# First q, k, v gradient tiles of a dense stage fetched while attention ends, weights partly issued by GpSimd, and copies of the last forward pair on ScalarE

## The chip, the cores and the metric

The kernel runs on one core of a Trainium2 chip. The metric is the device time of one execution in microseconds (us). The kernel before was run four times: 2415.22, 2419.77, 2419.97 and 2423.10 us, with a median of 2419.87.

## What is computed

The reference runs four residual layers forward over a sequence of 2048 rows with width 640, and then the gradients of all inputs for a given output gradient. Layers 0 and 2 are linear attention (A), layers 1 and 3 are sliding-window softmax attention with a window of 256 (B). The two A layers share weights, as do the two B layers. There are 32 heads of 20 columns.

```python
def _A_ref(x, wqkv, wo):
    ...
    pq, pk = phi(q), phi(k)
    kv = jnp.einsum("bhsd,bhse->bhde", pk, v)
    ...
    o = num / den
    return (lambda x, *d: x.transpose(*d))(o, 0, 2, 1, 3).reshape(B, S, D) @ wo

def _B_ref(x, wqkv, wo):
    ...
    mask = (idx[:, None] - idx[None, :] >= 0) & (idx[:, None] - idx[None, :] < W)
    scores = jnp.where(mask[None, None], scores, -1e9)
    p = _softmax(scores, axis=-1)
    o = jnp.einsum("bhqk,bhkd->bhqd", p, v)
    return (lambda x, *d: x.transpose(*d))(o, 0, 2, 1, 3).reshape(B, S, D) @ wo
...
x = x + _A_ref(_layernorm(x, axis=-1), A_wqkv, A_wo)
x = x + _B_ref(_layernorm(x, axis=-1), B_wqkv, B_wo)
x = x + _A_ref(_layernorm(x, axis=-1), A_wqkv, A_wo)
x = x + _B_ref(_layernorm(x, axis=-1), B_wqkv, B_wo)
```

The outputs are the last x and the gradients of the input, of the two qkv weights and of the two output weights.

## The kernel before

The sequence is cut into 16 tiles of 128 rows. Everything is unrolled in Python. Most instructions on an engine may be put in an order that the compiler's scheduler chooses, but a transfer that is "pinned" stays behind what was written before it for the same engine.

**Stages, in order of time.** The q, k, v products of layer 0 come first. Then come two forward pairs (`seg_pair`, layers 0 and 1, then 2 and 3). A pair runs the attention scores of layer B as the backbone: 16 row tiles with 8 groups of 4 heads each. For every unit, TensorE makes the scores (L412), ScalarE the exponentials (L418), GpSimd masks the edges (L421, L424), and TensorE multiplies by v (L440). Between them a plan feeds pieces of the row-wise work: `mix`, `proj1`, `qkv`, `proj2`. In the last pair two more are in the plan: `fetch_g` transposes a tile of the output gradient on TensorE and copies it from PSUM into `gT`; `do` multiplies it by the transposed weight (L811). In the middle of each row tile `flip_some` also transposes 128 columns of a weight on TensorE, copies them from PSUM into `flip_t` (L201) and stores them to HBM as `WT_d`, for the backward stages. `steady[0]` is true from the first unit of the row loop up to the last, and false before and after. The PSUM banks of all this row-wise work come from one pool of four (`d` in the profile), so a transpose on TensorE waits until an earlier bank has been copied out.

Then comes the backward pass: attention of layer 3 (about 832 to 1211 us), the dense stage of layers 3 and 2 (1211 to 1500), attention of layer 1 (1500 to 1971), the dense stage of layers 1 and 0 (1971 to 2224), and the rest of the weight gradients (to the end).

**Attention backward** (`seg_attention_bwd`) runs 8 groups of 4 heads by 16 row tiles, 128 units, and five steps more to empty its pipeline. In step s, TensorE makes the scores of unit s (L903), ScalarE its exponentials (L917), GpSimd masks them (L921, L925), and VectorE makes ds of the unit before (L937). Half of ds is transposed by a DMA from SP into `dsT`, the other half on TensorE (L947) and copied out (L950). In step s the products of unit s - 5 (L963) read dsT and give the q, k, v gradients `dqkv_o`, which are evacuated (L996) and stored to `dqkv` in HBM, four row tiles in one transfer from GpSimd's queue. A filler puts weight-gradient products of other layers (L1039) into the same PSUM bank; when its last one has been handed out it calls `late` (layer 3) or `done` (layer 1). These give the filler's SBUF pools back and queue the 26 weight tiles of the next dense stage: 15 of `WT`, 5 of `WoT`, 6 of `mbdT`, each 160 KB.

**Queues.** SP issues the loads and all DMA transposes (L152) in the order written. `drip(n)` takes n waiting loads off a list and pins them on SP at the start of a step: 3 in the first 16 steps, then 2, then 4 from step 112 on. `flush` issues waiting stores from GpSimd's queue (both show as L125).

**The dense stage** (`seg_dense_bwd`) starts when attention has ended. What is left in the list is issued, then per row tile `fetch` loads five tiles two steps ahead, the first of them a DMA transpose of `dqkv` into `dqkvT`; `dh0` and `dh1` multiply it by `WT` in 30 matmuls (L771); ScalarE and VectorE make the layer-norm gradient `car` (L779 to L788); TensorE transposes it; `dO` follows. The pool of `dqkvT` lies in memory that attention used, so the first transpose also waits for attention's last evacuation.

Of the kernel before, what the change touches and what calls it, by code (L numbers as in the profile page):

```python
# [14 lines left out]
BF = mybir.dt.bfloat16  # L15
F32 = mybir.dt.float32
P = 128
# [6 lines left out]
class Kern:  # L24
# [111 lines left out]
        while self.stores:  # L136
            self.dma(*self.stores.pop(0), self.nc.gpsimd)

    def drip(self, n, pin=True, queue=None):
        queue = self.queue if queue is None else queue  # L140
        while queue and (n > 0 or callable(queue[0])):
            x = queue.pop(0)
            if callable(x):
                x()
                continue
            x = self.dma(*x, self.nc.sync)
            if pin:
                self.tc.keep_in_program_order(x)
            n -= 1
# [339 lines left out]
    def seg_pair(self, l, acc, on_tail=None):  # L489

        nc, TT, H, G = self.nc, self.TT, self.H, self.G
        with ExitStack() as st:
# [7 lines left out]
            last = l + 2 > 3  # L500
# [8 lines left out]
            for i in range(2):  # L509
                s = pW.tile([P, 2 * H * HP], BF, name=f"qk_slab{i}")  # L510
# [3 lines left out]
            for i in range(5):  # L514
                s = pW.tile([P, H * HP], BF, name=f"v_slab{i}")
# [6 lines left out]
            steady = [False]  # L522
# [10 lines left out]
            bank = Bank()  # L533
# [39 lines left out]
            if last:  # L573
                WoT = pW.tile([P, self.DT, self.D], BF, name="WoT1")
                gr, gT, o3 = {}, {}, {}

            def fetch_g(t):
                if t == 0:
                    self.tr(WoT, self.Wo[1])
                if t == 0:  # L580
                    gr[0] = self.rows_in(pw.tile([P, self.D], BF, name="g_ld"), self.grad_out[0:P, :])
                if t + 1 < TT:
                    gr[t + 1] = self.rows_in(pw.tile([P, self.D], BF, name="g_ld"),
                                            self.grad_out[(t + 1) * P:(t + 2) * P, :])
                gT[t] = pw.tile([P, self.DT, P], BF, name="gT", bufs=1)
                self.flip(gr.pop(t), self.DT, gT[t], bank, [nc.vector.tensor_copy])
                yield 640

            def do(t):
# [23 lines left out]

            def nc_eng():
                turn[0] += 1
                return nc.vector.tensor_copy if steady[0] or turn[0] % 2 else nc.scalar.copy

            def pieces():
# [35 lines left out]
            n = len(units)  # L654
            AHEAD, LAG = 1, 2
            evs, it, done = {}, None, 0
            for u in range(-AHEAD, n + LAG):
# [9 lines left out]
                if 0 <= u < n:  # L667
# [3 lines left out]
                    for i, f in enumerate((1 / 3, 2 / 3, 1)):  # L671
                        self.flush()
                        while done < work * (g + f) / G:
                            w = next(it, None)
# [27 lines left out]
            if last:  # L702
                drain(fetch_g(TT - 1))
# [148 lines left out]
        self.tc.add_manual_dep(x.ins, y.ins.name, mybir.DependencyInfo(  # L852
            mybir.DependencyClass.NoSync, mybir.DependencyReason.DATA), reason="order")

    def seg_attention_bwd(self, l, fill):


        nc, T, TT, D, G = self.nc, self.T, self.TT, self.D, self.G
# [6 lines left out]
        with ExitStack() as st:  # L865
# [141 lines left out]
            n = len(units)  # L1007
            for s in range(n + JL):
                self.att_step = s
                self.flush()  # L1010
                self.drip(3 if s < TT else 2 if s < n - TT else 4)
                self.drip(2 if s < TT else 3, True, self.queue2)
                if s < n and units[s][1] == 3 and units[s][0] + 1 < G:
                    load(units[s][0] + 1)
                a, b2, c = s, s - PL - 1, s - PL
                bank = ahead() if 0 <= s - JL < n else None
                sa = scores(a, 0, "QT", "KT") if a < n else None
                pb = scores(b2, 1, "dOT", "VT") if 0 <= b2 < n else None
                if a < n:
                    expo(a, 0, sa)  # L1020
                if 0 <= b2 < n:
                    dscore(b2, 1, pb)
                if bank:
                    job(s - JL, *bank)
                sb = scores(a, 1, "QT", "KT") if a < n else None
                pa = scores(c, 0, "dOT", "VT") if 0 <= c < n else None
                if a < n:
                    expo(a, 1, sb)
                if 0 <= c < n:
                    dscore(c, 0, pa)  # L1030
                if 0 <= b2 < n:
                    flip(b2)
# [125 lines left out]
        return dmbd, dmbdT  # L1158

    def dense_weights(self, l, pool):  # L1160
        w = [self.load_w(pool, 1, "WT"), self.load_w(pool, 0, "WoT"), pool.tile([P, 6, self.D], BF, name="mbdT")]
        self.later([(w[2][:, k, :], self.sv[l - 1]["mbdT"][:, k, :]) for k in range(6)])
        return w

    def seg_dense_bwd(self, l, w, mid):

        nc, TT, D, DT, H, HD = self.nc, self.TT, self.D, self.DT, self.H, self.HD
# [3 lines left out]
        with ExitStack() as st:  # L1171
# [7 lines left out]
            with ExitStack() as s2:  # L1179
                p1 = self.pool(s2, "b1")  # L1180
                p1w = self.pool(s2, "b1w", 2)
                pl = self.pool(s2, "b1l", 3)
                WTB, WoTA, mbdT = w
                WTA = WoTB = None
                pps = self.pool(s2, "ps", 2, PSUM)
                pbd = self.pool(s2, "psb", 1, PSUM)
# [5 lines left out]
                dT, hn, g, o, pq, ps, gT, dN, dNT, dq = ({} for _ in range(10))  # L1192

                def fetch(t):
                    dT[t] = pl.tile([P, self.QTT, P], BF, name="dqkvT")
                    self.tr(dT[t], self.dqkv_d[l][:, t, :])
                    hn[t] = self.rows_in(pl.tile([P, D], BF, name="hn_ld"), self.hn_d[l][:, t, :])
                    g[t] = self.rows_in(pl.tile([P, D], BF, name="g_ld"), self.g_d[l][:, t, :])
                    o[t] = self.rows_in(pl.tile([P, D], BF, name="o_ld", bufs=4), self.o_d[a][:, t, :])
                    pq[t] = self.rows_in(pl.tile([P, D], BF, name="pq_ld", bufs=5), self.tm(sv["pq"])[:, t, :])  # L1200
# [65 lines left out]
            with ExitStack() as s2:  # L1266
                p2 = self.pool(s2, "b2")
                p2w = self.pool(s2, "b2w", 2)
                pl = self.pool(s2, "b2l", 3)
                pps = self.pool(s2, "ps", 3, PSUM)  # L1270
                hn, o, pk, pkT, vT, ps, gT, dkv, dkvT = ({} for _ in range(9))
# [123 lines left out]
    def run(self):  # L1395
        s_att = self.ctx.enter_context(ExitStack())
        with ExitStack() as st:
# [18 lines left out]
            for l in (0, 2):  # L1416
                self.seg_pair(l, acc, None if l == 0 else tail)
                self.drip(len(self.queue))
                if l == 0:
                    sA.close()  # L1420
        own = 6
        s_wg, last = ExitStack(), []
        with ExitStack() as s2:
            w = []

            def late():
                s_own.close()
                w.extend(self.dense_weights(3, self.pool(s2, "pre", side="right")))

            def mid():  # L1430
                s2.close()
                self.load_A(1)
                c0 = own * 12 * DH
                jobs = [(self.hn_d[3], self.dqkv_d[3], (c0, self.QT), self.part[1][0]),
                        (self.o_d[3], self.g_d[3], (0, self.D), self.part[1][1]),
                        (self.hn_d[2], self.dqkv_d[2], (0, self.QT), self.part[0][0]),
                        (self.o_d[2], self.g_d[2], (0, self.D), self.part[0][1])]
                last.append(self.fill_dram(s_wg, jobs, done))

            s_own = ExitStack()  # L1440
            self.seg_attention_bwd(3, self.fill_own(3, s_own, own, late))
            s_end, s3 = self.ctx.enter_context(ExitStack()), ExitStack()
            w1 = []

            def done():
                s_wg.close()
                w1.extend(self.dense_weights(1, self.pool(s3, "pre", side="right")))
            self.seg_dense_bwd(3, w, mid)
        fill = last[0]
        self.seg_attention_bwd(1, fill)  # L1450
        if fill.left:
            with ExitStack() as s2:
                ps = self.pool(s2, "wgp", 2, PSUM)
# [9 lines left out]
        last = []  # L1463
# [69 lines left out]
```

## Time and profile before

| | |
|---|---|
| median of 4 runs | 2419.87 us |
| profiled execution | 2414.3 us, span 2412.6 us |
| mean granted TensorE clock | 0.931 |
| TensorE (PE) busy | 2145.1 us, 89% |
| VectorE (DVE) busy | 1552.8 us, 64% |
| ScalarE (ACT) busy | 1242.6 us, 52% |
| GpSimd (POOL) busy | 1147.6 us, 48% |
| moved by DMA | 472.07 MB, 196 GB/s |

Stage by stage (window sums of the same execution):

| window, us | stage | PE busy | DVE | ACT | POOL | DMA share |
|---|---|---|---|---|---|---|
| 600 to 660 | last forward pair | 54.4 | 50.6 | 43.7 | 49.3 | 0.95 |
| 1160 to 1206 | attention of layer 3 ends | 40.1 | 32.1 | 29.1 | 19.8 | 0.81 |
| 1206 to 1216 | seam to dense | 4.1 | 2.8 | 1.5 | 1.9 | 0.56 |
| 1940 to 1976 | attention of layer 1 ends, seam | 21.6 | 17.9 | 13.5 | 10.6 | 0.92 |
| 1976 to 2115 | dense, first half | 126.7 | 89.5 | 48.1 | 50.4 | 0.73 |

A line of the profile names the engine, the line of the kernel (L771 is line 771), the operation and its tiles as out<-in. Busy time is not a limit in itself: an engine at 80% with a queue in fixed order can be late for the others, and one at 50% on which everything waits can set the time. The slices of the page are a fortieth of the span, 60.3 us each. SPq and POOLq are the queues in which SP and GpSimd issue transfers; the time shown for such an instruction is that of issuing it.

### The profile page before, as it was taken

What the parts mean: (1) busy time and instruction counts of PE and PEld (TensorE: products, weight loads), DVE (VectorE), ACT (ScalarE), POOL (GpSimd) and SP (SyncE); (2) the same over time, 40 slices, a digit from 0 to 9 for tenths busy, and PEclk for the clock granted to TensorE, in tenths of its full rate; (3) what the DMA queues carried; (4) which work ended last, traced back from release to release, by engine and by line L of the source; (5) the groups of instructions that cost most, each with busy time, mean ns of one, the idle gap of its engine ahead of it and who ended that gap; (6) DMA issues with size and microseconds to landing.
All of it is one profiled execution on the core that took longest, in us unless ns stands there. A gap on an engine that the chain in (4) does not pass through costs nothing. (4 is left out here: it accounts for less than half of the span.)

```text
span 2412.6 us, 68804 instructions
## 1 busy us (share of the span) xinstructions
PE 2145.1 (89%) x27568; PEld 1494.4 (62%) x27672; DVE 1552.8 (64%) x3022; ACT 1242.6 (52%) x1971; POOL 1147.6 (48%) x1779
## 2 busy tenths in 40 slices
PE   7879999879988699999889798889999979889989
PEld 4645565545555357777667575567777757667445
DVE  6657777567888568778756586556666656646112
ACT  4447777637767557777623353545666633333000
POOL 4447676557877536666433243445555533311000
PEclk9989999989999759999799998789999989989999
DMA  8599898488989798889798695999989999497797
GB/s 254 149 186 216 185 196 189 128 181 203 215 190 199 196 242 164 143 146 167 160 220 219 143 251 167 250 213 188 186 182 201 177 206 232 124 269 203 198 279 210
DMA packets 814817, 472.07 MB, mean 196 GB/s; under 512 B 609664, under 2 KB 781872, under 8 KB 814496
## 3 DMA queue, kind: packets, MB, share of 16 engines
q1 hardware_dynamic: 772880, 336.42, 67.8%
q0 software_dynamic: 41616, 131.25, 17.0%
q8 instruction: 216, 3.54, 0.6%
q14 instruction: 105, 0.86, 0.1%
HBM read 187.07 MB, written 161.19 MB: 144 GB/s over the span
## 5 line engine op out<-in xcount | busy, mean ns | idle before, releaser
L937 DVE SCALAR_TENSOR_TENSOR ds<-sp,e 128x768 bf16<-128x768 f32 (+2 forms) x512 | 463.0, 906 | 244.6 <-PE sp L903 151.3
L917 ACT ACTIVATE e<-sp 128x768 bf16<-128x768 f32 (+2 forms) x512 | 395.1, 776 | 257.7 <-PE sp L903 182.8
L418 ACT ACTIVATE e<-s 128x1024 bf16<-128x1024 f32 x360 | 364.8, 1024 | 115.6 <-PE s L412 69.7
L412 PE MATMUL s<-qbd,ring 128*128 128x512 bf16 x616 | 211.6, 387 | 6.6 <-ACT e L418 2.3
L921 POOL TENSOR_SCALAR_AFFINE_SELECT e<-e 128x512 bf16<-128x512 bf16 x256 | 164.6, 643 | 110.4 <-ACT e L917 101.2
L1039 PEld LDWEIGHTS <-wg_l 128*128 128x128 bf16 x2800 | 187.5, 99 | 42.9 <-DVE wg_o L1045 12.8
L903 PE MATMUL sp<-KT,QT 32*128 32x384 bf16 (+2 forms) x1024 | 186.0, 348 | 17.9 <-ACT e L917 10.9
L421 POOL TENSOR_SCALAR_AFFINE_SELECT e<-e 128x512 bf16<-128x512 bf16 x256 | 170.3, 667 | 47.9 <-ACT e L418 46.3
L903 PE MATMUL sp<-VT,dOT 32*128 32x384 bf16 (+2 forms) x1024 | 182.3, 344 | 9.5 <-ACT e L917 6.2
L1378 PE MATMUL wg<-wg_r,wg_l 128*128 128x480 bf16 (+1 forms) x960 | 177.4, 347 | 7.0 <-DMA wg_r<-dqkv 5.3
L1039 PE MATMUL acc<-wg_r,wg_l 128*128 128x160 bf16 x1840 | 157.3, 239 | 22.1 <-DMA wg_l<-o 6.1
L267 PE MATMUL d<-W,ln_hnT 128*128 128x320 bf16 x960 | 151.9, 307 | 25.5 <-ACT ln_hnT L730 8.7
L368 PE MATMUL d<-W,ln_hnT 128*128 128x480 bf16 x640 | 156.9, 377 | 4.8 <-DMA ln_hnT<-ln_hn 1.9
L771 PE MATMUL d<-WT,dqkvT 128*128 128x320 bf16 x960 | 144.7, 305 | 9.6 <-DMA dqkvT<-dqkv 5.0
L424 POOL TENSOR_SCALAR_AFFINE_SELECT e<-e 128x512 bf16<-128x512 bf16 x224 | 149.0, 665 | 8.7 <-ACT e L418 7.8
L1378 PEld LDWEIGHTS <-wg_l 128*128 128x128 bf16 x960 | 94.6, 99 | 89.7 <-issue 12.0
L440 PEld LDWEIGHTS <-e 128*128 128x128 bf16 x2880 | 109.9, 96 | 60.6 <-POOL e L421 22.8
L925 POOL TENSOR_SCALAR_AFFINE_SELECT e<-e 128x512 bf16<-128x512 bf16 x224 | 142.9, 638 | 0.0
L947 PE MATMUL tp<-ident,ds 128*128 128x128 bf16 x1440 | 137.1, 235 | 5.6 <-DVE ds L937 3.5
L267 PEld LDWEIGHTS <-ln_hnT 128*128 128x128 bf16 x960 | 94.3, 100 | 76.2 <-issue 20.6
L963 PEld LDWEIGHTS <-dsT 128*128 128x128 bf16 x2880 | 93.9, 98 | 69.7 <-issue 45.5
L440 PE MATMUL d<-v_slab,e 128*128 128x42 bf16 (+1 forms) x2880 | 116.2, 180 | 22.5 <-POOL e L421 19.2
(200 smaller groups left out, 4528.6 us busy)
## 6 DMA issues: line engine op xcount, KB each, us to landing
qkvT<-ring POOLq DMA_DIRECT2D x32, 512.0 KB, 5.3
dqkv<-dqkv_o POOLq DMA_DIRECT2D x64, 240.0 KB, 4.4
wg_r<-dqkv SPq DMA_DIRECT2D x64, 240.0 KB, 4.5
hn<-ln_hn SPq DMA_DIRECT2D x64, 160.0 KB, 2.9
qk<-qk_flat POOLq DMA_DIRECT2D x64, 160.0 KB, 4.0
qk_r<-qk SPq DMA_DIRECT2D x32, 320.0 KB, 4.2
hn_ld<-hn SPq DMA_DIRECT2D x64, 160.0 KB, 3.7
dqkv<-dkv_t POOLq DMA_DIRECT2D x32, 320.0 KB, 4.2
```

Source lines behind the costliest of these rows:

```text
L267: nc.tensor.matmul(ps, lhsT=hnT[:, k, :], rhs=W[:, k, ci * HD:(ci + 1) * HD], start=(k == 0), stop=(k == self.DT - 1))
L368: nc.tensor.matmul(ps, lhsT=hnT[:, k, :], rhs=W[:, k, ci * 480:(ci + 1) * 480], start=(k == 0), stop=(k == self.DT - 1))
L412: nc.tensor.matmul(ps[:, i, :], lhsT=self.ring_at(ring, 1, kt)[:, g, :], rhs=self.qbd[b % 2][:, g, :, :], start=True, stop=True)
L418: nc.scalar.activation(e[:, 0:i + 1], ps[:, 0:i + 1], ACT.Exp, scale=self.c_att)
L421: nc.gpsimd.affine_select(out=ev, in_=ev, compare_op=ALU.is_ge, fill=0.0, base=0, pattern=[[0, 4], [1, P]], channel_multiplier=-1)
L440: nc.tensor.matmul(ov[:, h % 16:h % 16 + w, :], lhsT=ev[i][:, hh, :], rhs=v[:, h:h + w, 0:DH + 1], start=(i == 0), stop=(i == nkt - 1), sk ...
L903: nc.tensor.matmul(ps[:, j, 0:nkt * P], lhsT=slabs[g][ta][r0:r0 + HP, b * P:(b + 1) * P], rhs=slabs[g][tb][r0:r0 + HP, k0 * P:(k0 + nkt) * P],
L917: nc.scalar.activation(ev[:, 2 * half:2 * half + 2], ps[:, :, 0:nkt * P].rearrange("p h (i k) -> p h i k", k=P), ACT.Exp, scale=c_att)
L921: nc.gpsimd.affine_select(out=ev[:, :, nkt - 1, :], in_=ev[:, :, nkt - 1, :], compare_op=ALU.is_ge, fill=0.0, base=0, pattern=[[0, 4], [-1 ...
L937: nc.vector.scalar_tensor_tensor(out=dv[:, hs], in0=ps[:, :, 0:nkt * P].rearrange("p h (i k) -> p h i k", k=P), scalar=c_att, in1=ev[:, hs ...
L1039: x = self.nc.tensor.matmul(ps[:, 0:w], lhsT=lhs(t), rhs=rhs(t), start=(t == 0), stop=(t == self.TT - 1), skip_group_check=True)
L1378: nc.tensor.matmul(ps, lhsT=lhs[:, tt, rows], rhs=rhs[:, tt, 0:w], start=(tt == 0), stop=(tt == TT - 1))
```

## The change

Three edits:

1. In the last forward pair, `gT` is copied out of PSUM by ScalarE, no longer by VectorE, and so is `flip_t` while `steady[0]` holds. 16 and 15 copies of 128x640 bf16 change their engine.
2. In attention backward, from step 112 on, `drip` issues three loads from SP and then one more from GpSimd's queue, in place of four from SP.
3. The tiles `dqkvT` 0 of layer 3, and 0 and 1 of layer 1, are allocated together with the weights of the dense stage. Their DMA transposes are issued by SP at the start of step 126, two steps before the last unit's scores, ahead of that step's loads. `fetch` then leaves them out for these tiles.

```diff
-    def drip(self, n, pin=True, queue=None):
+    def drip(self, n, pin=True, queue=None, eng=None):
...
-            x = self.dma(*x, self.nc.sync)
+            x = self.dma(*x, eng or self.nc.sync)
...
-                self.flip(gr.pop(t), self.DT, gT[t], bank, [nc.vector.tensor_copy])
+                self.flip(gr.pop(t), self.DT, gT[t], bank, [nc.scalar.copy])
...
             def nc_eng():
                 turn[0] += 1
+                if last and steady[0]:
+                    return nc.scalar.copy
                 return nc.vector.tensor_copy if steady[0] or turn[0] % 2 else nc.scalar.copy
...
-    def seg_attention_bwd(self, l, fill):
+    def seg_attention_bwd(self, l, fill, end):
...
-                self.drip(3 if s < TT else 2 if s < n - TT else 4)
+                if s == n - 2:
+                    end()
+                self.drip(3 if s < TT or s >= n - TT else 2)
+                if s >= n - TT:
+                    self.drip(1, True, None, nc.gpsimd)
...
-        w = [self.load_w(pool, 1, "WT"), self.load_w(pool, 0, "WoT"), pool.tile([P, 6, self.D], BF, name="mbdT")]
+        w = [self.load_w(pool, 1, "WT"), self.load_w(pool, 0, "WoT"), pool.tile([P, 6, self.D], BF, name="mbdT"),
+             [pool.tile([P, self.QTT, P], BF, name=f"dqkvT{i}") for i in range(1 if l == 3 else 2)]]
...
                 def fetch(t):
-                    dT[t] = pl.tile([P, self.QTT, P], BF, name="dqkvT")
-                    self.tr(dT[t], self.dqkv_d[l][:, t, :])
+                    if t < len(ahead):
+                        dT[t] = ahead[t]
+                    else:
+                        dT[t] = pl.tile([P, self.QTT, P], BF, name="dqkvT")
+                        self.tr(dT[t], self.dqkv_d[l][:, t, :])
...
+        def ahead(l, w):
+            for i, x in enumerate(w[3]):
+                self.tr(x, self.dqkv_d[l][:, i, :])
...
-            self.seg_attention_bwd(3, self.fill_own(3, s_own, own, late))
+            self.seg_attention_bwd(3, self.fill_own(3, s_own, own, late), lambda: ahead(3, w))
...
-        self.seg_attention_bwd(1, fill)
+        self.seg_attention_bwd(1, fill, lambda: ahead(1, w1))
```

More of the change, by code (lines that the diff above doesn't have):

```diff
@@ L1182, in seg_dense_bwd @@
                 pl = self.pool(s2, "b1l", 3)
-                WTB, WoTA, mbdT = w
+                WTB, WoTA, mbdT, ahead = w
                 WTA = WoTB = None
```

## The prediction

> **What bounds the kernel now.** I read the page first. Its slices show TensorE busy nearly everywhere and no one engine that is the limit of the whole, so the change has to be judged in the three places that it touches: the last forward pair, and the two seams from attention backward to dense backward (layers 3 and 1).
>
> ```profile
> PE   7879999879988699999889798889999979889989
> DVE  6657777567888568778756586556666656646112
> ACT  4447777637767557777623353545666633333000
> DMA  8599898488989798889798695999989999497797
> ```
>
> The last forward pair lies in slices 9 to 13 (about 545 to 812 us): PE is at 8 to 9 tenths, VectorE at 8, ScalarE at 6 or 7. DMA is at 9 almost everywhere.
>
> The second view is the chain that ended last, around the seam of layer 1.
>
> ```profile
> 1966.35 3.76 DMA dsT<-ds
> ...
> 1970.16 0.82 PE acc L963 x20
> ...
> 1971.10 4.69 DMA dqkvT<-dqkv
> ...
> 1975.93 6.04 PE d L771 x30
> ```
>
> The attention stage ends with the landing of its last dsT transpose (columns: start, length). Then the first tile of the dense stage is asked for, and TensorE stands until it is there. The timeline of PE at the layer-3 seam shows the same hole: the first product of the dense stage is
>
> ```profile
> 1216.11 10.70 PE L771 MATMUL d<-WT,dqkvT 128*128 128x320 bf16 x57 [4.66 <-issue]
> ```
>
> and its transpose was issued at 1211.59. The two holes, 4.66 and 4.96 us, lie on PE, and all that follows hangs on them.
>
> Third, SP's queue in the timeline before the layer-1 seam:
>
> ```profile
> 1945.83 1.76 SPq L125 DMA_DIRECT2D WT<-WT_d  x4
> ...
> 1949.08 2.02 SPq L125 DMA_DIRECT2D WT<-WT_d  x4
> 1951.20 1.78 SPq L152 DMA_TRANSPOSE dsT<-ds  x1
> ```
>
> A step costs SP four weight pieces at about 0.5 us and one transpose at 1.2 to 1.8, in all 3.3 us, while TensorE would step in 2.5 us (L963 at 1942.0, 1944.5, 1947.0, 1949.5). From 1945.8 to the last dsT, issued at 1966.35, SP therefore sets the pace.
>
> Fourth, what PE waits for in the forward window (the waits of PE, 545 to 812):
>
> ```profile
> PE d L728 <- DVE flip_t L201: 7.5, 7, 1.4
> PE d L440 <- POOL e L421: 6.3, 7, 2.0
> PE d L811 <- DVE car L253: 5.2, 5, 1.4
> ```
>
> Columns: total us, times, longest. VectorE being late costs PE more there than anything else.
>
> **What the skill says.** The Trainium skill, "DMA: Bandwidth & Descriptors", section "Issuing engines are not separate DMA queues": all issuing engines feed the same 16 DMA engines, and a second one saves only sequencer time. The trace agrees that the sequencer is worth saving (0.44 to 0.58 us a piece on SP) and warns that little else is: the DMA engines are busy 0.92 of 1940 to 1976. The same page, section "SWDGE vs HWDGE vs iDMA": a plain DMA transpose can't be issued from GpSimd; so only weights can leave SP. "VectorE: DVE Perf Modes", section "Specifications", has ScalarE closer to PSUM; here the copy of 128x640 bf16 out of PSUM takes 476 ns on VectorE (gT) and 692 ns on ScalarE (ln_hnT), so ScalarE is not the faster one, only the freer one.
>
> **The change, part by part.**
>
> *1. Copies to ScalarE.* 16 gT copies and 15 flip_t copies in the steady part go over. VectorE loses 31 x about 0.46 = 14 us, ScalarE gains 31 x 0.692 = 21 us. Over the 267 us that makes VectorE 0.81 to 0.75 and ScalarE 0.71 to 0.79 (window sums). What counts is PE's wait. Around a typical row (flip_t at 576.06) PE had finished its transposes about 2 us earlier, VectorE got to the copy only behind slow qbd copies, bn_stats and ln_mv, and PE then stood 1.19 us because the next flip needs that PSUM bank. ScalarE was idle for 2.35 us just then. So most of the 7.5 us should go, and the freed VectorE brings the car and o_b additions forward by up to 0.9 us a row, perhaps half of their 5.2 + 2.8 us: 11 us of relief. Against it stand the exponentials behind a copy, 0.69 us late each, some of which will reach PE through the GpSimd masks (the 6.3 us row grows). I take 5 us for that: **-6 us**. From both sides: -12 (all waits on VectorE go) to +10 (each copy delays PE by a third of a us).
>
> *2. Weights from GpSimd, layer 3.* 26 weight pieces come 3 + 1 per step from SP and GpSimd, so SP issues some 20. A dsT goes out 0.5 us earlier in a step, and up to 3.5 us over seven if nothing else holds it. PE waits for dsT there at 1173.20 (1.99 us), 1184.87 (2.37) and 1188.18 (0.16): 4.5 us are to be had. But SP also waits 6.1 us for VectorE's ds in 1160 to 1190, and the 4.06 us that four WoT pieces took at 1177.09 looks like a full queue rather than issue cost. **-2 us** (0 to -4.5). GpSimd pays 0.55 us a piece (its own 160 KB stores, g<-car, take 0.55 to 0.60) and has gaps of about 1 us a step: nothing, while those gaps last.
>
> *3. First tile ahead, layer 3.* One transpose (SP 1.3 to 2.9 us) two steps before the end. SP waits for ds between its last nine transposes (20.9 us for 9, against 1.2 of issue), so it fits in; it lands long before 1211. The hole of 4.66 goes. Next in line is the second tile, still fetched after the stage begins: four row loads (2.0 us), then the transpose (4.3 to 5.4 to landing) makes about 7 us, against 6.1 us of PE on the first tile. 0.9 us stays: **-3.8 us**.
>
> *4. The same at layer 1, two tiles.* The hole of 4.96 goes; the third tile has 12 us of PE ahead of it: **-4.9 us**. But here SP is full. Moving six pieces before the last dsT saves 6 x 0.5 = 3.0 us; the two transposes, put ahead of three dsT, cost 2.6 (unblocked) to 5.6 us, and their 2 x 480 KB compete with weights at about 200 GB/s, up to 5 us more for a dsT behind them. I take **+1.5 us** for the end of attention (-1 to +5).
>
> *5. The new wait.* SP's first weight waits for the last gradient store to land,
>
> ```profile
> SPq L125 <- DMA po0w<-wg_o: 2.2, 1, 2.2
> ```
>
> and 0.9 us at layer 3. GpSimd's first piece must wait for the same memory; behind it stand the two affine_selects of that step, and VectorE's ds waits for them: about 2 us late at layer 1. The cover is SP, which from there on is later than that anyway. If SP were quicker than I think, this wait would be what is late next.
>
> The sum is -6 - 2 - 3.8 - 4.9 + 1.5 = **-15.2 us**. The profiled execution took 2414.3 us (span 2412.6); it would become 2399.1. It lies 5.6 us under the median of 2419.87, so on the scale of the median I say **2405**.
>
> **Rivals.** *(a) The copies bring nothing*: PE's waits change their name from VectorE to ScalarE. For it: ScalarE runs exponentials of 1024 ns back to back in many rows. Against it: in the rows at 576, 634, 653, 673 and 736 us it was idle for 0.5 to 2.35 us just before ln_lv. The rest gives -9.2: 2411. *(b) The seams give back what they save*: with DMA at 0.92, prefetched tiles and weights delay the dsT that end the stage (+5 at layer 1, 0 at layer 3). With the copies and the holes -9.7: 2410; without the copies too, 2416. *(c) Slower: ScalarE becomes what PE waits for.* A flip_t copy queues behind ln_lv, which waits for VectorE's ln_mv, and an exponential; PE's next flip then waits up to 1.0 + 0.69 us, in 13 rows 22 us. Less the 9.2 of the seams that is +13: 2433. It decides from 9.2 us, or 0.3 us for each of the 31 copies. The idle ScalarE at those moments speaks against it. *(d) The change doesn't take effect*: the early transposes queue behind something on SP and land no earlier, and the waits pass from one engine to another: 2420, as now.
>
> **Numbers.** Main case 0.60 (its own range 2397 to 2412), (a) 0.17, (b) 0.10, (c) 0.09, (d) 0.04. The range that leaves out 2 in 10 is 2395 to 2418. A change under 0.2%, 4.8 us, can't be told from none here. Faster by more than that: the main case nearly whole (0.58), most of (a) (0.13), half of (b) (0.05), together 0.76. Slower: (c) and a little of (d), 0.11. Within: 0.13.
>
> **What would show it.** Right: no DMA wait ahead of the first L771 product at either seam; WT pieces in POOL's queue at about 0.55 us; flip_t and gT as ScalarE copies of 0.69 us, the PE wait on flip_t much under 7.5 us and the exponentials' wait on PE not much grown; dsT at the end of layer 1 issued within 2 us of before. Wrong: a PE wait of several us on dsT at the end of attention, POOL's affine_selects late with VectorE waiting, or the forward window longer than before with PE waiting for ScalarE.

## The result, and the profile after

| | runs | median, us |
|---|---|---|
| before, same chip | 56 | 2419.65 |
| after | 37 | 2416.35 |

The ratio is 0.9984, with a 95% interval of 0.9973 to 0.9994. Of 2419.65 us that is 3.9 us less (1.5 to 6.5), where 15 were forecast. The profiled execution of after took 2417.2 us (span 2415.4, mean granted TensorE clock 0.933), which is 2.9 us *longer* than that of before. A single profile scatters by several us, so stretches are compared here, not spans, and each stretch over more than one kernel.

The slices of the page are nearly those of before:

```profile
PE   6879999879898689999989797879999979889999
DVE  6657777567877557778766586556666656656212
ACT  4447777647777557777723343545666533333000
DMA  8599898489997799889998695999889999597797
```

**The last forward pair.** The waits of PE from 545 to 812 us, the longest five (total us, times, longest):

```profile
PE d L251 <- DVE o_t L347: 9.8, 8, 2.4
PE d L730 <- DVE o_b L446: 5.9, 4, 2.3
PE d L440 <- DVE car L253: 3.4, 8, 0.7
PE s L412 <- ACT e L418: 2.1, 3, 1.8
PE d L440 <- POOL e L421: 2.0, 4, 0.9
```

The wait on flip_t, 7.5 us before, is gone. So is most of the one on GpSimd. But PE's waits on VectorE add up to 21.3 us, against 18.7 before: other tiles of VectorE's are now what PE stands for, above all o_t, the output of layer A's attention. The timeline of after shows how, in the same place that the prediction had taken as typical (start, length, in brackets the idle time before and what ended it):

```profile
573.78 2.63 DVE L399 COPY qbd<-ring 32x1024 bf16<-32x1024 bf16 x2
...
574.79 0.69 ACT L201 COPY flip_t<-d 128x640 bf16<-128x640 bf16 x1
...
576.45 0.49 DVE L217 BATCH_NORM_STATS2 ln_st<-car 128x6 f32<-128x320 bf16 x1
...
577.46 0.89 DVE L347 TENSOR_TENSOR o_t<-d,rinv 128x320 bf16<-128x320 f32 x2
...
578.00 0.84 PE L251 MATMUL d<-Wo,oT 128*128 128x320 bf16 x5 [1.54 <-DVE o_t L347]
```

The copy is made on ScalarE at 574.79, and nobody waits for it. VectorE still spends 2.63 us in two copies of q into the operand `qbd` of the scores (one takes 0.40 us at its shortest), then does the layer-norm statistics, and only then o_t. PE stands 1.54 us for o_t, where it had stood 1.19 us for flip_t.

**The seam of layer 3.** PE's timeline, first products of the dense stage:

```profile
1211.33 0.70 PE L773 MATMUL d<-WT,dqkvT 128*128 128x320 bf16 x4
1212.68 0.70 PE L773 MATMUL d<-WT,dqkvT 128*128 128x320 bf16 x4
1213.77 3.15 PE L773 MATMUL d<-WT,dqkvT 128*128 128x320 bf16 x22
1221.34 4.76 PE L773 MATMUL d<-WT,dqkvT 128*128 128x320 bf16 x24 [4.42 <-DMA dqkvT<-dqkv]
```

The hole before the first product has gone: the products even start between the last ones of attention. A hole of nearly the same length, 4.42 us, stands ahead of the second tile, which landed 7.3 us after attention's end.

**The seam of layer 1.** SP's queue:

```profile
1947.70 1.21 SPq L152 DMA_TRANSPOSE dsT<-ds  x1
1948.95 1.56 SPq L125 DMA_DIRECT2D WT<-WT_d  x3
1950.61 5.72 SPq L152 DMA_TRANSPOSE dqkvT<-dqkv  x1
1956.43 2.21 SPq L152 DMA_TRANSPOSE dsT<-ds  x1
1958.69 1.52 SPq L125 DMA_DIRECT2D WT<-WT_d  x3
1960.31 2.23 SPq L152 DMA_TRANSPOSE dsT<-ds  x1
1962.58 3.12 SPq L152 DMA_TRANSPOSE dqkvT<-dqkv  x1
```

The three weights of a step now cost about 1.5 us, as meant. But the early transposes hold SP for 5.72 and 3.12 us, and the compiler's scheduler (the planner, from here on), free to move them since they are not pinned, put one of them ahead of five dsT and the other ahead of three (the last three dsT are issued behind the lines shown). On PE two of the groups of products that need a dsT are late:

```profile
1963.62 0.55 PE L965 MATMUL acc<-qk_r,dsT 128*128 128x40 bf16 x12 [6.56 <-DMA dsT<-ds]
...
1971.74 0.56 PE L965 MATMUL acc<-qk_r,dsT 128*128 128x40 bf16 x12 [3.95 <-DMA dsT<-ds]
```

And the chain that ended last goes on, behind the end of attention (start, length, what):

```profile
1973.82 3.26 DMA dsT<-ds
...
1977.79 6.67 PE d L773 x49
1984.45 4.78 issue
1989.24 0.69 PE t L730 x5
```

No transfer stands before the first product any more, but PE waits 4.78 us before the first transpose of `car`. What it waits for is in the timeline of the other engines:

```profile
1980.95 0.79 ACT L781 ACTIVATE dh_s<-d,rs 128x640 f32<-128x640 f32 x1 [5.02 <-PE d L773]
...
1982.77 3.30 POOL L1151 MEMSET dmbd<- 128x3840 bf16 x1 [3.21 <-issue]
1983.01 3.24 DVE L1254 TENSOR_SCALAR dphi<-pq_ld 128x640 bf16<-128x640 bf16 x1 [4.78 <-DMA g_ld<-g]
1986.17 0.81 DVE L784 CUSTOM_DVE_ANT_0 dh_junk<-dh_s,hn_ld 128x640 bf16<-128x640 f32 x1
...
1988.02 0.32 DVE L1254 TENSOR_SCALAR dphi<-pq_ld 128x640 bf16<-128x640 bf16 x1
```

ScalarE's dh_s is ready at 1981.8. The next step for `car` is dh_junk on VectorE, but the planner put dphi ahead of it: an operation for a later piece of the tile, which waits for the row load pq_ld (landed at 1982.88; the mark in the line names a load that had landed earlier) and then takes 3.24 us beside a memset of GpSimd's. The next one of the same shape takes 0.32.

### The profile page after: what moved, and what is told of

Its sections match the earlier page's. It is cut to its first block, busy times and chain, and to the rows that moved or that the text cites. A ratio compares the mean times of both kernels' runs of the same rounds, so it can differ in the third digit from the quotient of the medians.

```text
span 2415.4 us, 68820 instructions
## 1 busy us (share of the span) xinstructions
PE 2145.5 (89%) x27566; PEld 1495.0 (62%) x27672; DVE 1553.0 (64%) x2991; ACT 1261.1 (52%) x2002; POOL 1155.3 (48%) x1791
## 4 chain that ended last, share of the span: by engine, by line
PE 37%; DMA 9%; issue 6%; DVE 4%; POOL 3%; SPq 3%; ACT 2%; DVEq 0%; ACTq 0%; POOLq 0%
PE acc L965 7%; PE acc L1045 7%; PE d L773 6%; PE wg L1388 5%; PE sp L905 5%; PE tp L949 3%; SPq L125 2%; POOL do_o L753 2%; DMA dsT<-ds 2%; PE t L730 2%; ACT e L919 1%; DVE ds L939 1%; DVE car L790 1%; PE d L738 1%; DMA dqkvT<-dqkv 1%
## 5 line engine op out<-in xcount | busy, mean ns | idle before, releaser
L1045 PEld LDWEIGHTS <-wg_l 128*128 128x128 bf16 x2800 | 189.5, 100 | 46.1 <-DVE wg_o L1051 16.1
L905 PE MATMUL sp<-VT,dOT 32*128 32x384 bf16 (+2 forms) x1024 | 181.2, 342 | 10.1 <-ACT e L919 6.4
L440 PEld LDWEIGHTS <-e 128*128 128x128 bf16 x2880 | 110.3, 97 | 59.3 <-POOL e L421 18.0
L965 PE MATMUL acc<-qk_r,dsT 128*128 128x40 bf16 (+1 forms) x2880 | 118.4, 181 | 21.4 <-DMA dsT<-ds 20.8
```

The source lines that it names most:

```text
L905: nc.tensor.matmul(ps[:, j, 0:nkt * P], lhsT=slabs[g][ta][r0:r0 + HP, b * P:(b + 1) * P], rhs=slabs[g][tb][r0:r0 + HP, k0 * P:(k0 + nkt) * P],
L965: x.append(nc.tensor.matmul(acc[:, hh * DH:hh * DH + w], lhsT=lhsT, rhs=rhs(rname, g, t, hh, w), start=(i == 0), stop=(i == len(s) - 1), s ...
L1045: x = self.nc.tensor.matmul(ps[:, 0:w], lhsT=lhs(t), rhs=rhs(t), start=(t == 0), stop=(t == self.TT - 1), skip_group_check=True)
```

## The experiments

The marks used: "end" is the last product of attention backward, counted from the end of the last filler product, which is the last work that the change leaves alone; "car" is the first transpose of `car` on PE, from the end of attention or, as "tail", from that filler product. All are us of one profile. Every kernel was timed against before on the same chip; ratios carry their 95% interval. The kernels e1, e2, e3 and e5 share one chip, e7, e9, e10 and e11 a second, e12, e13 and e14 a third, so a difference between two ratios may cross chips. Three ratios rest on few executions (6 of e7, 9 of e10, 10 of e13), the others on 14 or more.

| kernel | ratio | layer 3: end, car, tail | layer 1: end, car, tail | PE waits for dsT, layer 1 |
|---|---|---|---|---|
| before | 1 | 54.5, 15.8, 70.3 | 31.7, 15.1, 46.8 | 8.8 |
| after | 0.9984 (0.9973 to 0.9994) | 50.5, 12.0, 62.6 | 36.5, 11.5, 47.9 | 12.4 |
| e1_copies | 0.9984 (0.9959 to 1.0009) | 51.7, 15.6, 67.3 | 30.4, 15.1, 45.5 | 7.8 |
| e2_ahead | 0.9996 (0.9983 to 1.0010) | 51.7, 13.6, 65.3 | 34.7, 9.8, 44.5 | 7.0 |
| e3_gpsimd | 0.9982 (0.9969 to 0.9995) | 49.4, 17.0, 66.4 | 28.0, 15.5, 43.6 | 5.2 |
| e5_dphi | 0.9968 (0.9953 to 0.9983) | 49.4, 12.6, 62.0 | 37.0, 7.1, 44.1 | 12.2 |
| e4_pinned | 0.9970 (0.9954 to 0.9986) | 49.4, 12.8, 62.2 | 35.2, 10.1, 45.4 | 11.1 |
| e11_actq | 1.0023 (1.0009 to 1.0037) | 53.3, 12.1, 65.4 | 40.4, 10.3, 50.7 | 2.1 |
| e7_late_dphi | 0.9947 (0.9927 to 0.9967) | 48.2, 11.5, 59.7 | 29.6, 12.8, 42.4 | 6.5 |
| e9_late | 0.9947 (0.9933 to 0.9962) | 47.7, 11.6, 59.3 | 30.8, 13.3, 44.1 | 4.5 |
| e10_second | 0.9954 (0.9933 to 0.9975) | 48.8, 14.1, 62.9 | 27.9, 12.5, 40.3 | 5.8 |
| e12_late_nocopies | 0.9968 (0.9950 to 0.9986) | 50.0, 12.0, 62.0 | 29.3, 13.4, 42.7 | 6.5 |
| e13_bytes | 0.9957 (0.9933 to 0.9980) | 48.7, 12.4, 61.1 | 32.6, 12.9, 45.5 | 9.1 |
| e14_late_gT | 0.9961 (0.9946 to 0.9977) | 48.7, 12.8, 61.5 | 31.6, 13.0, 44.5 | 7.1 |

### One part alone

*e1_copies*: the kernel before with the two edits to the copies, and nothing else of the change.

```diff
-                self.flip(gr.pop(t), self.DT, gT[t], bank, [nc.vector.tensor_copy])
+                self.flip(gr.pop(t), self.DT, gT[t], bank, [nc.scalar.copy])
...
+                if last and steady[0]:
+                    return nc.scalar.copy
```

> The kernel before with the 31 copies of the last forward pair on ScalarE and nothing else. Theory W (the waits only change their name): PE no longer waits for flip_t (7.5 us before) but as long for o_t, o_b and car, which VectorE makes late as ever, so PE's waits on VectorE in the forward window stay at 17 to 22 us and the time is 0.999 to 1.001 of before. Rival (the prediction): PE's waits fall by 6 us or more, ratio 0.9975. Rival (ScalarE now in the way): PE waits for ScalarE grow by over 5 us, ratio 1.002 or more.

*e2_ahead*: the early transposes alone, four weights a step on SP as before.

> The kernel before with the early dqkvT transposes alone (four weights a step from SP, copies as before). Theory S (SP is held): at layer 1 the two transposes take 8 to 9 us of SP's time among the last dsT, attention there ends 5 to 8 us later relative to the last filler product, and the seam gains 3 to 4 us at each layer: ratio 0.999 to 1.001. Rival (the prediction's sizes): the end of attention moves by 1 to 2 us only, ratio 0.997. Rival (GpSimd's weights are what delays dsT): without them the tail is as before, ratio 0.996.

*e3_gpsimd*: the weights alone, three a step on SP and one on GpSimd, nothing fetched early.

```diff
-                self.drip(3 if s < TT else 2 if s < n - TT else 4)
+                self.drip(3 if s < TT or s >= n - TT else 2)
+                if s >= n - TT:
+                    self.drip(1, True, None, nc.gpsimd)
```

> The kernel before with one of four weight pieces a step from GpSimd and nothing else. Theory S: SP's part of a step falls from 3.3 to 2.8 us, the last dsT of layer 1 goes out 2 to 3 us earlier relative to the last filler product, and the layer-3 tail gains 1 to 2 us; ratio 0.998 to 0.9995. Rival (GpSimd's weights hold its masks up or crowd the DMA engines): the last dsT no earlier or later, ratio 1.000 or more.

The weights from GpSimd alone (0.9982) bring as much as the whole change, and they help at layer 1 too, where the end comes at 28.0 in place of 31.7 and 30.4; the six kernels of the table that have these weights and fetch nothing early lie at 27.9 to 31.6, with a mean of 29.5. (That a second issuing engine saves sequencer time, as the section of the Trainium skill quoted in the prediction has it, was here worth about 1.5 us at the end of layer 1 and 2.6 to 3.5 at that of layer 3.) The early transposes alone bring nothing that can be measured (0.9996): at layer 1 the seam gains 5.3 us (car 9.8 for 15.1) and attention ends 3 to 4 us later, with 4.7 us of SP's time spent on the two. The copies alone are not told from nothing (0.9984, the interval holds 1). The waits of PE on VectorE in e1's forward pair show the same names as after:

```profile
PE d L251 <- DVE o_t L347: 7.2, 7, 1.5
PE d L730 <- DVE o_b L446: 5.4, 4, 2.3
PE d L440 <- DVE car L253: 3.9, 8, 0.7
```

### The seam of layer 1: dphi, the transposes, or both

*e5_dphi*: the kernel after with one VectorE operation kept in the order written.

```diff
-                    nc.vector.tensor_scalar(out=f, in0=q, scalar1=-1e-6, ...)
+                    x = nc.vector.tensor_scalar(out=f, in0=q, scalar1=-1e-6, ...)
+                    if t == 0:
+                        self.tc.keep_in_program_order(x)
```

> The changed kernel, with the dphi instruction of row tile 0 of each dense stage kept behind the vector work that is written before it, so that it no longer stands ahead of the first layer-norm gradient. Theory D (dphi, waiting for pq_ld and slowed beside GpSimd's memset, holds the first dh_junk back): the first car transpose comes 3.5 to 4.5 us sooner after the end of attention at each seam (12.0 and 11.3 us after the change, 15.8 and 15.0 before), ratio 0.995 to before. Rival (the row loads hn_ld and g_ld are as late, or later work swallows it): under 1.5 us at each seam, ratio 0.998 as with the change itself.

The end of attention stays (37.0), and car comes at 7.1 in place of 11.5. In the timeline dh_junk now follows dh_s at once, although the memset begins at the same point of the seam:

```profile
1964.60 0.80 ACT L781 ACTIVATE dh_s<-d,rs 128x640 f32<-128x640 f32 x1 [5.07 <-PE d L773]
...
1965.51 0.82 DVE L784 CUSTOM_DVE_ANT_0 dh_junk<-dh_s,hn_ld 128x640 bf16<-128x640 f32 x1 [3.64 <-ACT dh_s L781]
...
1966.48 3.30 POOL L1151 MEMSET dmbd<- 128x3840 bf16 x1 [3.28 <-issue]
1966.58 0.89 DVE L789 SCALAR_TENSOR_TENSOR dh_u<-hn_ld,dh_ab,dh_s 128x640 f32<-128x640 bf16 x1
```

So dphi took 4.4 us of what the removed hole had given, by the profiles; in time the kernel differs from after by 0.0016 (± 0.0018), which is not clear of noise. The Trainium skill, "SBUF — State Buffer", section "Who interferes with whom", says that VectorE and GpSimd share a port pair which one instruction holds to its end, and that a tensor_scalar is among those that can ask for it. The 3.24 us of dphi in after, which end 0.2 us behind the memset, agree. At layer 3 it took nothing (12.6 against 12.0): there the second tile is the later one.

*e4_pinned*: the kernel after, with the early transposes pinned, so that both stand directly ahead of the last three dsT, as the prediction had assumed.

```diff
-                self.tr(x, self.dqkv_d[l][:, i, :])
+                self.tc.keep_in_program_order(self.tr(x, self.dqkv_d[l][:, i, :]))
```

> The kernel after with its early transposes pinned where the text of the change puts them: at layer 1 both directly one behind the other ahead of the last three dsT on SP, where the prediction had assumed them (in the kernel after the planner put one ahead of five dsT and one ahead of three). If the planner's freedom is what went wrong: attention ends at +31 to +33 us from the last filler product (after: +36.5 and +37.0; transposes behind the last dsT: +27.9 to +31.6), ratio 0.995 to 0.9965. If two 15-block transposes ahead of any dsT are what costs: end at +34 to +38, PE's wait on dsT over 9 us, ratio 0.997 to 0.9985.

It meets the second expectation, the ratio only just: 0.9970, with the end at 35.2 and 11.1 us of waiting for dsT. The two transposes hold SP for 6.75 us:

```profile
1956.34 6.75 SPq L152 DMA_TRANSPOSE dqkvT<-dqkv  x2
```

Behind them one group of dsT products on PE is 7.30 us late. So the planner's freedom cost one to two us of the end, no more than single profiles scatter; that two such transposes stand ahead of any dsT at all is the rest. (In this kernel the planner also happened to put dphi behind dh_junk, though still ahead of the next operation for `car`, so a part of the 0.9970 may be dphi's.)

*e9_late*: pinned as in e4, and put behind the last dsT. *e7_late_dphi* is the same with dphi in order too.

```diff
-                if s == n - 2:
+                if s == n + 1:
                     end()
```

> As the one above but dphi left to the planner: the kernel after with the early transposes pinned behind the last dsT. If VectorE's dphi is what is late next only where PE comes early: attention ends at +28 to +30 as above, dphi waits for pq_ld again, and the first car transpose is 2 to 5 us later than in the kernel with dphi pinned (+43 to +47); ratio 0.997 to 0.999. If dphi no longer matters once the tile comes 2 us after attention's end (PE later, as before the change): the same +41 to +43.

> The kernel after with dphi pinned, and the early transposes pinned just behind the last dsT on SP, in place of three to four steps before the end. SP theory: layer 1's attention ends at +28 to +30 us from the last filler product as with the GpSimd weights alone (+28.0; with the early transposes +36.5 and +37.0), PE's wait on dsT is 5 us, the first product of the dense stage starts about 2 us after the end of attention (4.4 us before it where the tile lies ready), the first car transpose at +41 to +43: some 2 us better than with dphi alone (+44.1), ratio 0.995 to 0.997. Transfer theory: the same here, since the bytes are asked for later too; it is told apart by the run with ScalarE's queue. A third, that layer 1's tail is longer for a reason outside SP (PE order): end stays at +35 or more.

Both reach 0.9947, twelve to thirteen us under before. Against after, e9_late is lower by 0.0037 (± 0.0018), some 9 us (5 to 13), each taken against before on its own chip: what placing and pinning the transposes so is worth is clear of noise in the timed runs alone. Against e4_pinned, from which only the place differs, it is 0.0023 (± 0.0022), just clear of it. (A small part of the 13 us has a rival: the mean granted TensorE clock was 0.938 in e9's executions and 0.936 in those of before on that chip, and among the latter an execution is on the mean about 1 us shorter for each 0.001 of clock. That would make some 2 us.) Attention ends at 30.8 and 29.6. SP's queue in e9_late:

```profile
1958.06 1.43 SPq L152 DMA_TRANSPOSE dsT<-ds  x1
1959.59 4.22 SPq L152 DMA_TRANSPOSE dqkvT<-dqkv  x2
```

and PE's timeline there:

```profile
1964.57 10.45 PE L773 MATMUL d<-WT,dqkvT 128*128 128x320 bf16 x57 [1.24 <-DMA dqkvT<-dqkv]
```

PE pays 1.24 us there for the tile, of the 4.96 that stood before. The same at layer 3: the first product starts 0.7 to 0.9 us after attention's end, and the second tile then costs 2.10 us in e9 and nothing in e7. The order of dphi now matters little (first car at 13.3 without it, 12.8 with it, and the same ratio), which is nearer to the second expectation for e9, though 44.1 from the filler product lies above its 41 to 43: with the first products 5 us later at the seam, dphi's wait for pq_ld lies mostly under them.

*e13_bytes*: e9 and, at layer 1, two plain copies of the same rows into the same tiles at the place where the change had its transposes. The late transposes overwrite what they write.

> The kernel after with the early transposes pinned behind the last dsT, and two plain copies of the same 480 KB rows into the same two tiles put on SP ahead of three dsT at layer 1, where the change had its transposes; the late transposes overwrite them. They move the same bytes at the same place, for about 0.5 us of SP each instead of 3 to 6. If SP's issue of the transposes is what the end of attention paid for: it ends +30 to +32 us from the last filler product, as without the copies (+30.8, +29.6, +27.9), PE waits for dsT 4 to 7 us, ratio 0.994 to 0.9955. If it is the bytes beside the dsT and the weights: end at +34 to +37, PE waits over 9 us, ratio 0.9965 to 0.998.

Attention ends at 32.6 where five kernels without early bytes lie between 27.9 and 31.6 (mean 29.8), and three with early transposes at 35.2, 36.5 and 37.0. The copies took SP 1.0 us. One dsT behind them was long in landing:

```profile
1951.57 9.44 DMA dsT<-ds
```

So neither theory is shown to hold alone. Of some 6.4 us that the early transposes cost (mean 36.2 less 29.8), about 2.8 come with the bytes, of which 1.0 is SP's issue, and about 3.6 only with transposes. These are single profiles, which lie up to 3.7 us apart for kernels without early bytes, and the ratio (0.9957) can't decide it.

What the profiles do show is where the time sits. From the last filler product to the last dsT, SP's issues add up to 25.7 to 29.3 us in the three kernels with early transposes and to 19.1 to 21.8 in the six that have GpSimd's weights and nothing early; the last dsT lands at 34.5 to 36.3 us and at 27.0 to 30.7. In all fourteen kernels attention ends 0.7 to 1.0 us after that landing. So the products of the dense stage that PE already runs between the last ones of attention (eight of them at layer 1 in after) are not what makes its end late. Why a transpose's issue takes so much longer there is open.

*e11_actq*: e5 with the early transposes issued from ScalarE's queue.

```diff
-                self.tr(x, self.dqkv_d[l][:, i, :])
+                self.nc.scalar.dma_start_transpose(out=x, in_=self.dqkv_d[l][:, i, :])
```

> The kernel after with dphi pinned, and the three early dqkvT transposes issued from ScalarE's queue, at the same places in the steps; bytes, buffers and the time of asking are unchanged, only SP doesn't issue them. If SP's issue time is what the early transposes cost at layer 1: SP's last dsT goes out at +24 to +26 us from the end of the last filler product (+32.8 with the transposes on SP), attention ends at +28 to +31 (+37.0), PE waits for dsT at most 6 us (12.2), the first car transpose is at +36 to +39 (+44.1), and the ratio to before is 0.992 to 0.995. If it is the transfers instead (2 x 480 KB beside the dsT and the weights on the 16 DMA engines): dsT still lands late, attention ends at +34 or later, PE waits over 9 us for dsT, ratio 0.996 to 0.998. Between the two, if ScalarE's exponentials stand behind the issue: PE's and VectorE's waits on e grow by 2 to 6 us in the last steps. Layer 3 as before this edit (end +49, first car +12.6).

It is slower than before, and it doesn't tell issue from bytes, since the transposes of the two queues wait for one another. The Trainium skill, "DMA: Bandwidth & Descriptors", section "Silent corruption: two transposing streams in flight at once", asks for just that: the later stream has to wait until the earlier one has landed. The expectation had overlooked it. The waits of SP's queue at layer 1:

```profile
SPq L152 <- DMA dqkvT<-dqkv: 14.4, 2, 9.4
```

And ScalarE, which runs the exponentials, stands before its own transpose:

```profile
1943.05 0.35 ACT L998 CAST dqkv_o<-acc 128x240 bf16<-128x240 f32 x1
1952.01 1.85 ACTq L1437 DMA_TRANSPOSE dqkvT<-dqkv  x1
1953.91 0.81 ACT L919 ACTIVATE e<-sp 128x768 bf16<-128x768 f32 x1 [10.51 <-DMA WT<-WT_d]
```

The exponentials come 10.51 us late, PE waits 8.3 us for them, and attention ends at 40.4.

### The second tile at layer 3

*e10_second*: e7 with the second tile's transpose asked for behind one row load in place of four.

```diff
+                    for i in ([1] if l == 3 else []) if t == 0 else [t] if t not in dT else []:
                         dT[i] = pl.tile([P, self.QTT, P], BF, name="dqkvT")
-                        self.tr(dT[t], self.dqkv_d[l][:, t, :])
+                        self.tc.keep_in_program_order(self.tr(dT[i], self.dqkv_d[l][:, i, :]))
```

> As the kernel with dphi pinned and the transposes behind the last dsT, and at layer 3 the second tile's transpose asked for behind one row load of the first tile in place of four. If the second tile is what the layer-3 seam gives its gain back to: PE's wait of 4.4 to 4.7 us on dqkvT of tile 1 shrinks to 2 to 3 us, and the first car transpose comes 10 to 11 us after the end of attention (12.0 and 12.6 now); ratio 0.001 lower than its partner. If the wait is for the memory that attention frees or for the DMA engines: the tile lands no earlier and nothing moves. Layer 1 as its partner.

Nothing is gained: PE waits 2.05 us for the second tile, for which e7 had not waited at all, the first car comes at 14.1, and the ratio is that of e7 within its interval. The transpose was issued at 1204.71, 0.5 us after attention's end, and landed 8.3 us later; in e7, issued at 2.6 us, it had landed 4.8 us later, so that asking earlier made it land no earlier. Why is open.

### The copies once more

*e12_late_nocopies*: e9 without the copies' two edits. *e14_late_gT*: e9 with only the gT edit.

> The kernel after with the early transposes pinned behind the last dsT (0.9947 to before), and without the 31 copies on ScalarE: they stay on VectorE. If the copies are worth the 6 us that the prediction gave them: the ratio rises by 0.0025, to 0.997. If PE's waits only change their name (flip_t for o_t and o_b): the ratio stays at 0.9945 to 0.9955 and the forward window is as long within the scatter of single profiles. If ScalarE costs PE: below 0.994.

> The same base, with the 16 gT copies on ScalarE and the 15 flip_t copies left on VectorE. If the flip_t copies are where PE gains (their wait was 7.5 us in the kernel before): ratio 0.996 to 0.997 and PE's wait on flip_t is back at 6 to 8 us. If neither set of copies moves PE: 0.9945 to 0.9955 as with both and with none.

PE's forward waits show the old name again, in e12:

```profile
PE d L728 <- DVE flip_t L201: 7.2, 8, 1.3
```

and in e14:

```profile
PE d L728 <- DVE flip_t L201: 9.5, 9, 1.3
```

In time, e9 less e12 is 0.9947 - 0.9968 = -0.0021 (± 0.0023, the root of the sum of squares of the two half-widths), or -5 us with an interval that holds 0; the two were timed on different chips. e14 lies between. Taken together with e1, each weighted by its interval, it is -0.0019 (± 0.0017), some -5 us: timed runs alone speak for a gain, allow the forecast 6 us, and only just exclude none. The profiles say less: from the first gT copy to the first score product of attention backward, four kernels without the copies take 288.3 to 289.7 us (mean 288.9), and nine with both sets 286.8 to 290.5 (mean 288.2). PE's waits on VectorE from 545 to 812 us are 18.7 to 24.4 us without (mean 21.1) and 18.3 to 22.2 with (mean 19.9). What changes is the name: PE waits 7.2 to 11.4 us for flip_t and at most 0.3 for o_t in the four, and nothing for flip_t and 7.1 to 9.8 for o_t in the nine.

## Why the prediction was wrong

The forecast of 2405 us was 11 too low, and it took the wrong case as the likeliest. The step that failed is the price of the two early transposes at layer 1 (4 below): they held up the end of attention there by more than was reckoned, and the hole that they removed was in part filled by a late operation of VectorE's. A second term, the copies (1), was too large by an amount that stays open. In number the result is that of rival (b) together with (a), for which the text had worked out 2416. That it fits so well is in part luck: (b) put nothing for the weights at layer 3, which brought 2.6 to 3.5 us, and (a) had the waits pass to ScalarE, where they passed to another tile of VectorE's.

1. **Copies, -6: oversized.** "So most of the 7.5 should go" was right, and so was the freer ScalarE: flip_t took 0.69 us, gT 0.69, and no copy held up PE. What failed is the next step, "the freed VectorE brings the car and o_b additions forward", by half of their waits. VectorE was freed nearly as meant: its busy time from 545 to 812 us has a mean of 218.0 us in the four kernels without the copies and of 207.9 in the nine with both sets, 10 us less, where the copies that lie there had taken 12 to 13. But PE's wait of 8.4 us for flip_t became one of 8.2 for o_t, and those for car and o_b together went from 9.5 only to 8.8 (means over the same kernels). It looks as if PE waits for the end of a fixed row of VectorE operations, of which flip_t was one link. The 5 us set against the relief did not come either: PE's wait for GpSimd's masks fell from 5.0 to 3.0, that for ScalarE rose from 0.6 to 1.2. All waits of PE there fell by 2.5 us, and the profiles' windows give 288.2 - 288.9 = -0.7 us; the timed pairs e1 and e12 give -4 and -5, each with an interval that holds 0. The size between these stays open.

2. **Weights from GpSimd, -2 at layer 3: right, perhaps a little low.** The end at layer 3 has a mean of 52.6 in the three kernels without them (before, e1, e2) and 49.1 in the ten with them that leave ScalarE's queue alone: -3.5. A part of this may be the clock's: in that stretch of before's profile the mean granted clock was 0.69, in the other kernels 0.79 to 0.96. Against e1 and e2 alone (both 51.7) it is -2.6. PE's waits for dsT there fell too, from 5.0 to 6.1 us without to 1.8 to 3.9 with. At layer 1 the same, counted there as 3.0 saved on SP, is 31.0 (before and e1) less 29.5: half of it.

3. **First tile ahead, layer 3, -3.8: right in sum, wrong in its parts.** The first car comes at 15.8, 15.6 and 17.0 without it, at 12.0 to 13.6 with it (five kernels, mean 12.6): -3.5. But the second tile's wait was not 0.9 but 4.42 us. The tile itself landed 7.3 us after attention's end, close to the 7 of the prediction; the wait is longer because PE runs the first products from 2.6 us *before* that end on, which the sum had not counted as a gain.

4. **Layer 1, -4.9 + 1.5: the step that failed.** The term "two transposes cost 2.6 (unblocked) to 5.6 us" of SP measured 5.72 + 3.12 = 8.8 us (10.3 in e5_dphi, 6.75 in e4_pinned; 4.7, inside the range, in e2_ahead), and "put ahead of three dsT" was five and three. The end moved not by +1.5 but by +5.5 (36.5 less 31.0; the mean of the three such kernels gives +5.2), at the upper end of its range of -1 to +5 or just beyond. The hole's own term, -4.9, came out as -3.7 in car (11.5 less 15.2): "the third tile has 12 us of PE ahead of it" looked only at transfers, and VectorE's dphi was what came late next (e5_dphi: 7.1). With the transposes pinned behind the last dsT, e9_late takes 9 us (5 to 13) less than after, most of the 11.3 that the forecast missed.

5. **GpSimd's new wait: harmless, as forecast, and smaller.** Ahead of the first piece at layer 1 GpSimd idles 0.75 us, not 2, and the profile puts that down to a transpose of PE's and not to the store. The mask follows at once:

```profile
1946.14 0.56 POOL L125 DMA_DIRECT2D WT<-WT_d  x1 [0.75 <-PE tp L949]
1946.71 0.65 POOL L923 TENSOR_SCALAR_AFFINE_SELECT e<-e 128x512 bf16<-128x512 bf16 x1
```

The sum from the marks: -0.7 - 3.5 - 3.5 + 5.5 - 3.7 = -5.9 us, with the copies at the profile's value (-5.0 with -2.6 for the weights); measured -3.9 (-6.5 to -1.5). Of the 11.3 us that are missing from the forecast, layer 1 is 1.8 + 3.4 = 5.2, and the copies are most of the rest if their profile value holds. With the copies at the -4 to -5 of the timed pairs the marks don't add up to what was measured. Rival (c) is refuted: PE's waits on ScalarE grew from 0.8 to 2.1 us only. Rival (b) was named with the right mechanism and priced at +5, of which the prediction's main sum kept 1.5.

The two mistakes are of one kind. The holes that the trace showed were taken at their full length, and what would be late next was looked for among transfers only; and a step put into a queue that already set the pace was priced by issues from quieter moments of that queue.

The same sum with the transposes behind the last dsT (means over e7, e9, e10, e12 and e14): the end at layer 1 -1.2 (29.8 less 31.0), its car -2.2 (13.0 less 15.2), layer 3 -3.9 for the end (48.7 less 52.6) and -3.7 for car (12.4 less 16.1), the copies -0.7: -11.7 us, against a measured -0.0053 x 2412.55 = -12.8 in e9 (-16.2 to -9.2). This version is faster than both kernels.

## What to carry to other kernels

Where a prefetch is issued from a queue which already paces the stage, try it behind the last item that the stage waits for, even if that leaves a us of waiting: here 1.2 us of waiting for the tile was much cheaper than an end of attention that came 6 us later. After removing a stall, follow each engine's *order* through the next 10 us, not the transfers alone: the next late item may be an unrelated operation that the planner has put first because it used to have time. Where an engine with a fixed order is late as a whole, the wait for one of its tiles need not be the price of that tile: here 8.4 us for flip_t turned into 8.2 for o_t.

## What the runs showed of the hardware

- The issue of one DMA transpose of 480 KB (15 blocks of 128x128) on SP varied from 1.3 us (layer-3 seam of before) to 7.15 (among the last dsT and weights of layer 1 in e5_dphi); a plain copy of the same 480 KB took 0.42 to 0.54 in e13_bytes.
- A VectorE tensor_scalar on bf16 128x640 (dphi), alone 0.32 us, took 3.24 beside a 3.30 us GpSimd memset in after, 2.15 in e4_pinned and 1.91 in e9_late, and each time ended 0.2 us after the memset did, whenever it had begun. A tensor_scalar of 128x2 f32 (dh_ab), 0.15 in e4_pinned, took 0.83 in e7_late_dphi and ended with the memset. In e5_dphi dh_u, a scalar_tensor_tensor with f32 output, ran in its usual 0.89 beside it.
